# Four more attention pairs turned on VectorE instead of TensorE, in a kernel of attention and two feed-forward blocks

## The chip, the cores and the metric

The kernel runs on one core of a Trainium2 chip. The metric is the device time of one execution in microseconds, here the median of a few runs. The core has a matrix engine (TensorE, PE in the profile), three engines for elementwise work (VectorE is DVE, ScalarE is ACT, GpSimd is POOL) and DMA queues, which this kernel drives from SyncE (SP). Each engine works through its own instructions in a fixed order and waits on semaphores for what the others make.

## What is computed

```python
# attention: B, H, S, D = 4, 12, 448, 64, causal
scores = scale * np.matmul(q, k.transpose(0, 1, 3, 2))
scores = np.where(mask, -1000000000.0, scores)
scores = scores - np.max(scores, axis=-1, keepdims=True)
attn = np.exp(scores)
attn = attn / (np.sum(attn, axis=-1, keepdims=True) + 1e-09)
out = np.matmul(attn, v)
# x: 1792 tokens x 768
h = (x @ w1) * (x @ w2) @ w3          # 768 -> 1024 -> 1024
x = h @ w_out                         # 1024 -> 768
h = x @ w_in                          # 768 -> 2048
g = h - np.tanh(h)
out = g @ moe2_w_out                  # 2048 -> 768
```

All of it is in float32. The kernel forms w3 @ w_out once ("the product") and uses that for the second step.

## The kernel before

Large products keep each operand as two rounded parts, hi and lo, and take three matmuls for each step of the contraction (L411 to L413). `split` (L272) makes the parts: a cast gives hi on ScalarE or VectorE, and a subtraction gives lo on GpSimd or VectorE.

The work of attention goes by pairs of heads: a pair (b, p) is heads 2p and 2p + 1 of batch b, and there are six pairs in a batch. Two forms are in use. In the **first form** (`attention`, L432) TensorE makes the scores (L488) in chunks of 112 queries, VectorE adds the mask and finds the maximum (L459), ScalarE takes the exponential (L501), TensorE turns the probabilities by 20 matmuls with the identity (L513), they are copied out of PSUM to the tiles `pt`, TensorE multiplies with v (L541) and spreads the reciprocal sums (L548). The result goes through `xp` (L552, L554) and `split` (L557) into `x`, the input of the bilinear product. In the **turned form** (`turned`, L569) the scores (L657) come in two groups with rows of 64 to 448 columns, VectorE reduces (L603), ScalarE takes the exponential (L620), ScalarE or VectorE scales with the reciprocal (L629, L631), VectorE turns blocks of 32 x 32 (L633), and TensorE multiplies with v by 100 small matmuls in row groups of 32 (L683), which stand in two halves in the order. v is kept four times, once for each row group.

Before the change, the 12 pairs of batches 0 and 1 are in the first form and the 12 of batches 2 and 3 in the turned one; the outputs of batches 2 and 3 are stored to DRAM (`scx`, L700) and fetched in the second half of the kernel. The tiles of the turned form take the place of those of the first (the pools `at` and `bt`), so the first of them waits for the end of all first-form pairs.

Beside attention, TensorE works on one long sequence of other matmuls: the product (`product`, tiles mm<-g,hl), then, for the tokens of batches 0 and 1, the bilinear product with w1 and w2 (`bilinear`, L780, tiles mm<-x,hl) in blocks of 384 and 512 tokens (`BLOCKS`), then `project` (L816). The block of 384 needs x of batch 0 alone, the block of 512 x of both batches. Each step k of the contraction needs the x of pair k of the batch. The weights for these come raw from DRAM and are converted by `convert` (L288) on ScalarE, VectorE and GpSimd; `jobs_12` are w1 and w2, and the first `EARLY` = 4 tiles of w_in are converted in this first stage too.

The order of all this is made by a planner when the kernel is built (`Plan`, L89): each step has a rank and an estimated cost, and the step that can start first is taken. Pairs have ranks by their number, the long sequence has the last rank and fills what is left. On the chip only the order remains, with semaphores.

After this first half, the second half of the tokens and the two steps with w_in and w_out follow, in the same manner.

Of the kernel before, what the change touches and what calls it, by code (L numbers as in the profile page):

```python
# [25 lines left out]
B, H, S, D = 4, 12, 448, 64  # L26
NT, DM, FF, FF2 = 1792, 768, 1024, 2048
P = 128
CH = 112
NCH = S // CH  # L30
NKB = S // 32
NP = H // 2

EARLY = 4
W = 2 * S

# [17 lines left out]
def block(a, c):  # L54

    return (a if a < 2 else None) if c == 0 else 4 * c - 2 + a


def tokens():

    return [32 * block(a, c) + i for a in range(4) for c in range(4) if block(a, c) is not None for i in range(32)]

# [133 lines left out]
def act(n, psum=False):  # L198
    return "ACT", (0.104 if psum else 0.147) + n / 1400
# [31 lines left out]
def dma(size):  # L231
    return "DMA", max(0.5, size / 330e3)
# [3 lines left out]
def body(ctx: ExitStack, tc: tile.TileContext, qkd, vd, vd4, w12, w3t, wo, w_in, wo2, out):  # L236
    nc = tc.nc
    V, A, G, SP, PE = nc.vector, nc.scalar, nc.gpsimd, nc.sync, nc.tensor
    PSUM = bass.MemoryType.PSUM
    plan = Plan()  # L240
# [31 lines left out]
    def split(n, hi, lo, x):  # L272

        copy((yield [act(n), dve2(n)]), hi, x)
        sub((yield [pool(n), dves(n)]), lo, x, hi.bitcast(F32))
# [109 lines left out]
    scx = [dram.tile([P, W], F32, name=f"scx_{p}") for p in range(NP)]  # L385
# [43 lines left out]
    x_ready = grid(4, NP)  # L429
    spilled = grid(2, NP)  # L430

    def attention(at, aps, x_a):  # L432
        pairs = [(b, p) for b in range(2) for p in range(NP)]
        r_qk = Ring(at, [P, 2, S], F32, "qk", 2)
        r_v = Ring(at, [CH, NCH, 2, D], F32, "v", 2)
        r_p = Ring(at, [CH, 2, 1120], F32, "p", 2)
# [5 lines left out]
        qks, qk_at = {}, [Event() for _ in pairs]  # L442
        vs, v_at = {}, [Event() for _ in pairs]
        over = [Event() for _ in pairs]

        def load(ring, tiles, events, src):
            for n, (b, p) in enumerate(pairs):
                tiles[n] = yield ring
                yield dma(4 * P * 8 * D if tiles is vs else 4 * P * W)
                SP.dma_start(out=tiles[n].t, in_=src[b, p])  # L450
                plan.set(events[n])

        def scaled(p, st, chunks, ps, event):
# [112 lines left out]
        return over  # L566


    def turned(at, aps, pps):  # L569
        pairs = [(b, p) for b in range(2, B) for p in range(NP)]  # L570
        r_qk = Ring(at, [P, 2, S], F32, "qk", 3)
        r_v = Ring(at, [P, NKB, 2, D], F32, "v", 2)
        r_p = Ring(at, [P, 2, PLACE[-1]], F32, "p", 2)
# [2 lines left out]
        r_xb = Ring(at, [P, S], F32, "xb", 2)  # L576
        r_sc = Ring(aps, [P, 2, 512], F32, "sc", 1)
        r_pv = Ring(pps, [P, 4, 512], F32, "pv", 1)
        qks, qk_at = {}, [Event() for _ in pairs]
        vs, v_at = {}, [Event() for _ in pairs]  # L580
        over = [Event() for _ in pairs]

        def load(ring, tiles, events, src, first):
            for n, (b, p) in enumerate(pairs):
                tiles[n] = yield ring
                yield dma(4 * P * NKB * 2 * D if tiles is vs else 4 * P * W)
                SP.dma_start(out=tiles[n].t, in_=src[b - first, p])
                plan.set(events[n])

        def soft(p, pt, st, chunks, ps, rank, left, event):  # L590
# [46 lines left out]

        def pair(n):
            b, hp = pairs[n]
            rank = 24 + 2 * n  # L640

            yield qk_at[n]
            qk = qks.pop(n)
            p = yield r_p
            sb = yield r_st
            pt = yield r_pt
            left, event = [2 * 4], Event()
            for group in ((3, 0), (2, 1)):
                ps = yield r_sc
                yield wide(sum(WIDE[c] for c in group), 2)  # L650
                chunks, o = [], 0
                for c in group:
                    w = WIDE[c]
                    q0 = max(0, P * c - D)
                    for e in range(2):
                        d = slice(e * D, (e + 1) * D)
                        PE.matmul(ps.t[:, e, o:o + w], qk.t[d, 0, q0:q0 + P], qk.t[d, 1, :w], start=True, stop=True)  # L657
                    chunks.append((c, o))
                    o += w
                plan.spawn(soft(p, pt, sb.t, chunks, ps, rank, left, event), rank)  # L660
            plan.done(qk)

            yield event
            plan.done(p)
            plan.done(sb)
            yield v_at[n]
            v = vs.pop(n)
            ps = yield r_pv
            for kb in range(NKB):
                if kb in (0, 6):  # L670

                    if kb:
                        plan.pause(4.0)
                    yield "PE", 1.4
                for a in range(4):
                    have = [c for c in range(4) if block(a, c) is not None and block(a, c) >= kb]
                    if not have:
                        continue
                    r = slice(32 * a, 32 * a + 32)
                    for e in range(2):  # L680
                        src = pt.t[r, e, have[0] * STEP + kb * 32:]
                        x = bass.AP(tensor=src.tensor, offset=src.offset, ap=[src.ap[0], [STEP, len(have)], [1, 32]])
                        PE.matmul(ps.t[e * D:(e + 1) * D, a, have[0] * 32:P], v.t[r, kb, e], x,  # L683
                                  start=kb == 0, stop=kb == block(a, 4 - 1))
            plan.done(pt)
            plan.done(v)
            tk = slice((b % 2) * S, (b % 2 + 1) * S)

            def parts(t):

                return (t[:, :256].rearrange("p (a n) -> p a n", a=2), t[:, 256:].rearrange("p (a n) -> p a n", a=2))
            out = ps.t[:, 0:2, :P], ps.t[:, 2:4, 32:P]
            xb = yield r_xb
            o = parts(xb.t)
            for i in range(2):
                yield act(S // 2, True)
                A.copy(out=o[i], in_=out[i])
            plan.done(ps)
            yield dma(P * S * 4)
            SP.dma_start(out=scx[hp][:, tk], in_=xb.t)  # L700
            plan.set(spilled[b - 2][hp])
            plan.done(xb)
            plan.set(over[n])

        plan.spawn(load(r_qk, qks, qk_at, qkd, 0), 24)
        plan.spawn(load(r_v, vs, v_at, vd4, 2), 25)
        for n in range(len(pairs)):
            plan.spawn(pair(n), 24 + 2 * n)
        return over


# [275 lines left out]

    def start(cv, r_raw, r_t, at, aps):
        x = yield r_x
        xa["over"] = attention(at, aps, x.t)  # L990
        plan.spawn(first_half(cv, r_raw, r_t, x), plan.FILLER)
        plan.set(spawned)
# [9 lines left out]
        plan.run(xa["over"])  # L1002
    with tc.tile_pool(name="bt", bufs=1) as bt, tc.tile_pool(name="bps", bufs=1, space=PSUM) as bps, \
            tc.tile_pool(name="bpp", bufs=1, space=PSUM) as bpp:
        over = turned(bt, bps, bpp)
        plan.run([l1_over])
        plan.run(over + [j.stored for j in jobs_12 + jobs_in[:EARLY]] + sum(ab_ready[0], []))
    cv.__exit__(None, None, None)
# [105 lines left out]
```

## Time and profile before

| | before |
|---|---|
| median of 3 runs | 1066.53 us (1063.65 to 1068.56) |
| the profiled execution | 1062.6 us |
| its span | 1060.8 us |
| TensorE (PE) busy | 1036.4 us, 98% |
| VectorE (DVE) busy | 643.3 us, 61% |
| ScalarE (ACT) busy | 619.4 us, 58% |
| GpSimd (POOL) busy | 242.5 us, 23% |

The profile is of one execution, and its span is the time from the first to the last instruction; the execution's own time has 1.8 us more around it. The share of an engine is its busy time over the whole span. The chain that ended last is followed back from the last instruction, at each step to what released it; its pieces follow one another and add up to the span. Matmuls are pipelined, so the duration of one in a list is longer than the distance to the next.

### The profile page before, as it was taken

To read this page: it belongs to the slowest core of one execution; us is meant where nothing else is said; L and a number is where in the kernel's file an instruction comes from. 1 tells how busy PE (TensorE), PEld (TensorE's weight loads), DVE (VectorE), ACT (ScalarE), POOL (GpSimd) and SP (SyncE) were. 2 spreads that over 40 slices of the span, in tenths; PEclk is the share of its full clock that TensorE was granted. 3 is DMA by queue.
4 is the path that set the end of the run, shared out by engine and by line. 5 is a ranking of instruction groups with operands and counts; after the bars stand their busy time and mean duration, and the time that the engine had idled before them with its cause. 6 is when DMAs were issued, how large, how long until landed. Compare 5 with 4: busy or idle time off the path is not lost.

```text
span 1060.8 us, 19813 instructions
## 1 busy us (share of the span) xinstructions
PE 1036.4 (98%) x7680; PEld 899.3 (85%) x7680; DVE 643.3 (61%) x1316; ACT 619.4 (58%) x1353; POOL 242.5 (23%) x188
## 2 busy tenths in 40 slices
PE   5799999999999999999999999999999999999998
PEld 3577788778888989888998989899888988988987
DVE  7886556667665466656565377384756655474742
ACT  6997868788776243433432488573736556553620
POOL 3542131222223400124532022121111111121210
PEclk8999999999999999999999999999999999999999
DMA  7674449877764798999998333233333543233124
GB/s 265 205 215 161 121 149 315 298 255 253 251 223 159 295 366 301 347 323 319 354 326 300 142 118 119 90 129 109 109 110 117 167 140 115 92 120 117 44 87 155
DMA packets 72318, 209.03 MB, mean 197 GB/s; under 512 B 6113, under 2 KB 21473, under 8 KB 70689
## 3 DMA queue, kind: packets, MB, share of 16 engines
q1 hardware_dynamic: 72224, 207.77, 57.0%
q8 instruction: 60, 0.98, 0.4%
q14 instruction: 34, 0.27, 0.1%
HBM read 155.45 MB, written 52.30 MB: 196 GB/s over the span
## 4 chain that ended last, share of the span: by engine, by line
PE 91%; ACT 3%; DMA 2%; DVE 2%; issue 1%; POOL 0%; SPq 0%; ACTq 0%; DVEq 0%
PE mm L411 28%; PE mm L413 27%; PE mm L412 27%; PE pv L683 3%; PE sc L657 2%; PE att L541 1%; DMA raw<-w3t 1%; ACT p L501 1%; PE att L488 1%; PE att L513 1%; ACT pt L267 1%; ACT raw L304 1%; DVE p L459 1%; DMA qk<-qkd 1%; DVE t L321 0%
## 5 line engine op out<-in xcount | busy, mean ns | idle before, releaser
L411 PE MATMUL mm<-x,hl 128*128 128x384 f32 (+1 forms) x768 | 282.1, 367 | 0.0
L413 PE MATMUL mm<-x,hl 128*128 128x384 f32 (+1 forms) x768 | 278.8, 363 | 0.0
L412 PE MATMUL mm<-x,hl 128*128 128x384 f32 (+1 forms) x768 | 278.6, 363 | 0.0
L270 POOL TENSOR_TENSOR g<-g 128x384 fp32r<-128x384 f32 (+1 forms) x64 | 76.7, 1199 | 371.1 <-ACT g L267 371.1
L411 PEld LDWEIGHTS mm<-x,hl 128*128 128x128 f32 x768 | 144.1, 188 | 18.7 <-issue 2.0
L413 PEld LDWEIGHTS mm<-x,hl 128*128 128x128 f32 x768 | 144.1, 188 | 15.3
L412 PEld LDWEIGHTS mm<-x,hl 128*128 128x128 f32 x768 | 144.2, 188 | 14.7
L413 PE MATMUL mm<-g,w 128*128 128x384 f32 (+1 forms) x384 | 139.6, 364 | 0.0
L412 PE MATMUL mm<-g,w 128*128 128x384 f32 (+1 forms) x384 | 139.4, 363 | 0.0
L411 PE MATMUL mm<-g,w 128*128 128x384 f32 (+1 forms) x384 | 139.1, 362 | 0.0
L897 DVE SCALAR_TENSOR_TENSOR g<-r,g 128x512 f32<-128x512 f32 (+1 forms) x192 | 124.7, 659 | 20.4 <-ACT r L888 17.6
L888 ACT ACTIVATE r<-sq,cst 128x384 f32<-128x384 f32 (+1 forms) x192 | 123.6, 666 | 8.0 <-DVE g L897 8.0
L411 PE MATMUL mm<-g,hl 128*128 128x384 f32 (+1 forms) x320 | 116.3, 363 | 2.1 <-POOL g L270 2.1
L413 PE MATMUL mm<-g,hl 128*128 128x384 f32 (+1 forms) x320 | 113.0, 353 | 0.0
L412 PE MATMUL mm<-g,hl 128*128 128x384 f32 (+1 forms) x320 | 112.9, 353 | 0.0
L881 DVE SCALAR_TENSOR_TENSOR g<-sq,mm 128x384 f32<-128x384 f32 (+1 forms) x64 | 39.6, 619 | 109.2 <-ACT th L879 108.6
L314 DVE TENSOR_SCALAR t<-raw 128x512 uint32<-128x512 uint32 (+1 forms) x80 | 52.3, 654 | 69.6 <-DMA raw<-wo 39.1
L875 ACT ACTIVATE sq<-mm 128x384 f32<-128x384 f32 (+1 forms) x64 | 34.7, 543 | 92.5 <-PE mm L413 92.4
L304 ACT ACTIVATE raw<-raw 128x512 uint32<-128x512 uint32 (+1 forms) x80 | 63.9, 799 | 33.7 <-DMA raw<-wo 16.3
L270 POOL TENSOR_TENSOR hl<-t,hl 128x512 fp32r<-128x512 f32 (+1 forms) x32 | 52.1, 1635 | 134.0 <-ACT hl L267 99.1
L321 DVE CUSTOM_DVE_ANT_0 t<-raw,t 128x1024 uint16<-128x1024 uint16 (+1 forms) x80 | 75.1, 938 | 6.7 <-ACT raw L304 0.2
L412 PEld LDWEIGHTS mm<-g,w 128*128 128x128 f32 x384 | 72.1, 188 | 8.0
(81 smaller groups left out, 1599.0 us busy)
## 6 DMA issues: line engine op xcount, KB each, us to landing
hl<-sci SPq DMA_DIRECT2D x32, 768.0 KB, 4.6
w<-sco SPq DMA_DIRECT2D x48, 512.0 KB, 3.5
raw<-w SPq DMA_DIRECT2D x16, 768.0 KB, 5.7
sc<-hl SPq DMA_DIRECT2D x16, 768.0 KB, 4.4
raw<-w_in SPq DMA_DIRECT2D x16, 768.0 KB, 6.7
hl<-scp SPq DMA_DIRECT2D x12, 1024.0 KB, 6.5
hl<-sc SPq DMA_DIRECT2D x16, 768.0 KB, 7.0
raw<-wo SPq DMA_DIRECT2D x24, 512.0 KB, 6.7
```

Of the source, the lines that this page charges most:

```text
L270: (V if eng == "DVE" else G).tensor_tensor(out=out, in0=in0, in1=in1, op=ALU.subtract)
L304: A.activation(out=u, in_=u, func=AF.Copy, scale=2.0 ** -29)
L314: V.tensor_scalar(out=t, in0=raw[:, :n, 1], scalar1=3, scalar2=0x3FFFFFF8, op0=ALU.logical_shift_left, op1=ALU.bitwise_and)
L321: V.tensor_tensor(out=t, in0=t, in1=raw[:, :n, 0], op=ALU.add)
L411: PE.matmul(ps, wh, xl, start=k == 0, stop=False)
L412: PE.matmul(ps, wl, xh, start=False, stop=False)
L413: PE.matmul(ps, wh, xh, start=False, stop=k == last)
L683: PE.matmul(ps.t[e * D:(e + 1) * D, a, have[0] * 32:P], v.t[r, kb, e], x, start=kb == 0, stop=kb == block(a, 4 - 1))
L875: A.activation(out=sq, in_=h, func=AF.Square)
L881: V.scalar_tensor_tensor(out=g, in0=sq, scalar=LEAD, in1=h, op0=ALU.mult, op1=ALU.mult)
L888: A.activation(out=rk.t[:, :n], in_=sq, func=AF.Square, bias=cst[:, k:k + 1])
L897: V.scalar_tensor_tensor(out=g, in0=rk.t[:, :n], scalar=QUAD[k][1], in1=g, op0=ALU.add, op1=ALU.mult)
```

## The change

The first form now takes the first eight pairs only (`FIRST = 8`: batch 0 and pairs 0 and 1 of batch 1), and the turned form takes the other sixteen. The four turned pairs of batch 1 write their output through `split` into `x`, as the first form does, and the others are stored as before. The copy of a turned output from PSUM now puts the tokens in their natural order (64 and 384 elements in place of 256 and 192), so that the host need not reorder its result. The input arrays `vd` and `vd4` are cut at pair 8 in place of batch 2.

```diff
+FIRST = 8
...
     def attention(at, aps, x_a):
-        pairs = [(b, p) for b in range(2) for p in range(NP)]
+        pairs = [(b, p) for b in range(B) for p in range(NP)][:FIRST]
...
-                SP.dma_start(out=tiles[n].t, in_=src[b, p])
+                SP.dma_start(out=tiles[n].t, in_=src[n] if tiles is vs else src[b, p])
...
-    def turned(at, aps, pps):
-        pairs = [(b, p) for b in range(2, B) for p in range(NP)]
+    def turned(at, aps, pps, x_a):
+        pairs = [(b, p) for b in range(B) for p in range(NP)][FIRST:]
...
-            rank = 24 + 2 * n
+            rank = 2 * (FIRST + n)
...
-            out = ps.t[:, 0:2, :P], ps.t[:, 2:4, 32:P]
-            xb = yield r_xb
-            o = parts(xb.t)
-            for i in range(2):
-                yield act(S // 2, True)
-                A.copy(out=o[i], in_=out[i])
-            plan.done(ps)
-            yield dma(P * S * 4)
-            SP.dma_start(out=scx[hp][:, tk], in_=xb.t)
-            plan.set(spilled[b - 2][hp])
+            xb = yield r_xb
+            yield act(D, True)
+            A.copy(out=xb.t[:, :D].rearrange("p (a n) -> p a n", a=2), in_=ps.t[:, :2, :32])
+            yield act(S - D, True)
+            A.copy(out=xb.t[:, D:].rearrange("p (c a n) -> p a c n", a=4, n=32),
+                   in_=ps.t[:, :, 32:P].rearrange("p a (c n) -> p a c n", n=32))
+            plan.done(ps)
+            tk = slice((b % 2) * S, (b % 2 + 1) * S)
+            if b < 2:
+                yield from split(S, x_a[:, 0, hp, tk], x_a[:, 1, hp, tk], xb.t)
+                plan.set(x_ready[b][hp])
+            else:
+                yield dma(P * S * 4)
+                SP.dma_start(out=scx[hp][:, tk], in_=xb.t)
+                plan.set(spilled[b - 2][hp])
...
-        "vd": v[:2].reshape(2, NP, 2, NCH, CH, D).transpose(0, 1, 4, 3, 2, 5),
-        "vd4": np.tile(v[2:].reshape(2, NP, 2, NKB, 32, D).transpose(0, 1, 4, 3, 2, 5), (1, 1, 4, 1, 1, 1)),
+        "vd": v.reshape(B * NP, 2, NCH, CH, D)[:FIRST].transpose(0, 3, 2, 1, 4),
+        "vd4": np.tile(v.reshape(B * NP, 2, NKB, 32, D)[FIRST:].transpose(0, 3, 2, 1, 4), (1, 4, 1, 1, 1)),
```

Line numbers in the changed kernel are lower by 3 in the functions concerned (L411 is L408, L657 is L654, L683 is L680, L267 is L264, L620 is L617). Two places of the order matter below. The first is TensorE, where the first block of 512 tokens of the bilinear product begins (mm_2188 before). Before the change it stands between the first and the second turned pair of batch 2:

```order
L683 MATMUL pv_2009<-pt_1761,v_1745 64x32 x20
L411 MATMUL mm_2093<-x_163,hl_1809 128x384
L412 MATMUL mm_2093<-x_163,hl_1809 128x384
L413 MATMUL mm_2093<-x_163,hl_1809 128x384
L411 MATMUL mm_2188<-x_163,hl_1809 128x512
L412 MATMUL mm_2188<-x_163,hl_1809 128x512
L413 MATMUL mm_2188<-x_163,hl_1809 128x512
L683 MATMUL pv_2191<-pt_1778,v_1813 64x128 x4
```

In the changed order the block is mm_2106; its steps k = 0 to 4 stand between the output groups of the moved pairs, and this is its last step, k = 5, behind the last output of the fourth moved pair (pv_2187, which is pair 5 of batch 1) and one group of scores of a later pair:

```order
L680 MATMUL pv_2187<-pt_1892,v_1893 64x32 x20
L654 MATMUL sc_2344<-qk_1829 128x448 x2
L654 MATMUL sc_2344<-qk_1829 128x64 x2
L408 MATMUL mm_2106<-x_163,hl_1618 128x512
L409 MATMUL mm_2106<-x_163,hl_1618 128x512
L410 MATMUL mm_2106<-x_163,hl_1618 128x512
L408 MATMUL mm_2367<-x_163,hl_1812 128x512
```

What moved: the last step of the block reads x of a pair whose output is made directly ahead of it. The second place is ScalarE, where the x of pair 5 of batch 1 is cast to its hi part. Before, that is the first form (xp_1710), ahead of all turned pairs:

```order
L304 ACTIVATE raw_1619<-raw_1619 128x768
L552 COPY xp_1710<-att_1678 128x448
L267 CAST x_163<-xp_1710 128x448
L750 CAST res_1756<-mm_1686 128x384
L750 CAST res_1811<-mm_1755 128x384
L620 ACTIVATE p_1759,st_1760<-p_1759,st_1760 128x448 x2
```

In the changed order it is the turned form (xb_2335), among the exponentials (L617) and scalings (L626) of the next pair:

```order
L617 ACTIVATE p_1986,st_1988<-p_1986,st_1988 128x320 x2
L617 ACTIVATE p_1986,st_1988<-p_1986,st_1988 128x192
L687 COPY xb_2335<-pv_2187 128x64
L617 ACTIVATE p_1986,st_1988<-p_1986,st_1988 128x192
L689 COPY xb_2335<-pv_2187 128x4x3x32
L607 ACTIVATE st_1988<-st_1988 128x4
L264 CAST x_163<-xb_2335 128x448
```

What moved: the copies and the cast of this x are interleaved with the softmax of the next pair, and the subtraction for lo stays on GpSimd.

## Rows read from the trace of the kernel before

**Rows 1.** The page: its span, busy time by engine, and the chain by engine.
```profile
span 1060.8 us, 19813 instructions
...
PE 1036.4 (98%) x7680; PEld 899.3 (85%) x7680; DVE 643.3 (61%) x1316; ACT 619.4 (58%) x1353; POOL 242.5 (23%) x188
...
PE 91%; ACT 3%; DMA 2%; DVE 2%; issue 1%; POOL 0%; SPq 0%; ACTq 0%; DVEq 0%
```

**Rows 2.** What TensorE waited for, 95 to 345 us: total us, times, longest.
```profile
PE pv L683 <- issue: 1.0, 2, 0.7
```

**Rows 3.** The chain, 113 to 133 us, first form: start us, us, what.
```profile
116.58 1.92 PE att L513 x20
118.49 0.20 PE mm L411
...
119.56 2.08 PE att L488 x16
121.64 0.37 PE mm L411
122.01 0.17 PE mm L412
...
122.36 2.04 PE att L541 x16
124.40 0.53 PE att L548 x4
```

**Rows 4.** The chain, 206 to 236 us, turned form.
```profile
209.00 1.45 PE pv L683 x60
210.46 0.37 PE mm L411
...
216.56 0.43 PE mm L411
216.99 0.23 PE mm L412
...
217.46 1.12 PE sc L657 x8
...
223.19 1.06 PE sc L657 x8
```

**Rows 5.** Groups by line and form: busy us, mean ns, then idle before.
```profile
L620 ACT ACTIVATE p<-p,st 128x192 f32<-128x192 f32 x24 | 10.8, 449 | 2.3 <-DVE st L603 2.3
...
L270 POOL TENSOR_TENSOR x<-xp,x 128x448 fp32r<-128x448 f32 x12 | 15.7, 1311 | 51.5 <-ACT x L267 51.5
...
L267 ACT CAST x<-xp 128x448 fp32r<-128x448 f32 x12 | 6.9, 571 | 2.8 <-DVE xp L554 2.8
...
L697 ACT COPY xb<-pv 128x256 f32<-128x256 f32 x12 | 4.4, 370 | 3.9 <-PE pv L683 3.8
...
L697 ACT COPY xb<-pv 128x192 f32<-128x192 f32 x12 | 3.8, 317 | 0.0
```

**Rows 6.** The timeline of ScalarE and of GpSimd: start us, us, instruction, idle before.
```profile
152.76 0.57 ACT L267 CAST x<-xp 128x448 fp32r<-128x448 f32 x1 [0.69 <-DVE xp L554]
153.41 1.79 POOL L270 TENSOR_TENSOR x<-xp,x 128x448 fp32r<-128x448 f32 x1 [0.83 <-ACT x L267]
```

**Rows 7.** What ScalarE waited for, 95 to 360 us.
```profile
ACT raw L304 <- DMA raw<-w: 3.7, 3, 3.1
```

**Rows 8.** Windows of 1 us: length, PE busy, granted clock, DMA share, GB/s.
```profile
18.00:19.00 1.00, 0.04 (x2) 0.58 0.32 129
...
24.00:25.00 1.00, 1.00 (x5) 0.51 0.29 49
...
39.00:40.00 1.00, 0.00 (x0) 1.00 0.90 362
```

**Rows 9.** The chain: first output of the first turned pair, last of the fourth.
```profile
180.11 1.45 PE pv L683 x60
...
227.24 1.37 PE pv L683 x81
```

More of the change, by code (lines that the diff above doesn't have):

```diff
@@ L56, in block @@
     return (a if a < 2 else None) if c == 0 else 4 * c - 2 + a
-def tokens():
-    return [32 * block(a, c) + i for a in range(4) for c in range(4) if block(a, c) is not None for i in range(32)]
 class Event:
@@ L581, in turned, with load @@
         over = [Event() for _ in pairs]
-        def load(ring, tiles, events, src, first):
+        def load(ring, tiles, events, src):
             for n, (b, p) in enumerate(pairs):
@@ L586, in load @@
                 yield dma(4 * P * NKB * 2 * D if tiles is vs else 4 * P * W)
-                SP.dma_start(out=tiles[n].t, in_=src[b - first, p])
+                SP.dma_start(out=tiles[n].t, in_=src[n] if tiles is vs else src[b, p])
                 plan.set(events[n])
@@ L686, in pair @@
             plan.done(v)
-            tk = slice((b % 2) * S, (b % 2 + 1) * S)
-            def parts(t):
-                return (t[:, :256].rearrange("p (a n) -> p a n", a=2), t[:, 256:].rearrange("p (a n) -> p a n", a=2))
-            out = ps.t[:, 0:2, :P], ps.t[:, 2:4, 32:P]
-            xb = yield r_xb
-            o = parts(xb.t)
-            for i in range(2):
-                yield act(S // 2, True)
-                A.copy(out=o[i], in_=out[i])
-            plan.done(ps)
-            yield dma(P * S * 4)
-            SP.dma_start(out=scx[hp][:, tk], in_=xb.t)
-            plan.set(spilled[b - 2][hp])
+            xb = yield r_xb
[5 more added lines that the diff above has]
+            plan.done(ps)
+            tk = slice((b % 2) * S, (b % 2 + 1) * S)
+            if b < 2:
[5 more added lines that the diff above has]
+                plan.set(spilled[b - 2][hp])
             plan.done(xb)
             plan.set(over[n])
-        plan.spawn(load(r_qk, qks, qk_at, qkd, 0), 24)
-        plan.spawn(load(r_v, vs, v_at, vd4, 2), 25)
+        plan.spawn(load(r_qk, qks, qk_at, qkd), 2 * FIRST)
+        plan.spawn(load(r_v, vs, v_at, vd4), 2 * FIRST + 1)
         for n in range(len(pairs)):
-            plan.spawn(pair(n), 24 + 2 * n)
+            plan.spawn(pair(n), 2 * (FIRST + n))
         return over
@@ L989, in start @@
         x = yield r_x
+        xa["x"] = x.t
         xa["over"] = attention(at, aps, x.t)
@@ L1004, in body @@
             tc.tile_pool(name="bpp", bufs=1, space=PSUM) as bpp:
-        over = turned(bt, bps, bpp)
+        over = turned(bt, bps, bpp, xa["x"])
         plan.run([l1_over])
@@ L1111 @@
     o = r.results[0]["out"]
-    o = o.transpose(2, 0, 1).reshape(B, S, DM)
-    return np.concatenate([o[:2], o[2:, np.argsort(tokens())]]).reshape(NT, DM)
+    return np.ascontiguousarray(o.transpose(2, 0, 1).reshape(NT, DM))
```

## The prediction

> **What bounds the kernel now.** I read four things, in this order. The head of the page [rows 1] shows TensorE busy for 98% of the span and 91% of the chain that ended last; VectorE and ScalarE, by the same rows, work about six tenths of the time. A share over the whole span hides stages, so the second view is what TensorE waited for between 95 and 345 us, the stretch that holds the last attention pairs and all pairs that VectorE turns [rows 2]: 1.0 us of pauses in issue, ahead of two groups of pv matmuls, is the one entry that touches the turned pairs. In that stretch the span is the sum of what TensorE is given to do, and a microsecond of matmuls taken away is a microsecond of span as long as no wait appears. Third, the chain in that stretch gives the time that each kind of step takes of TensorE [rows 3, 4, 9]; its durations run from the start of one step to the start of the next, so they may be added, unlike the means of the page, which overlap. Fourth come the pieces off TensorE from which a new wait would be made [rows 5 to 7], and the granted clock after gaps [rows 8]. Before 95 us TensorE does wait, but the changed kernel issues the same matmuls in the same order until the output of pair 5 (counted from 0), so I carry that stretch over unchanged; and behind the last pv group the instructions of TensorE are again the same to the end.
>
> **The matmuls removed and added.** A pair in the first form costs TensorE 2.08 us of scores, 1.92 of transposes, 2.04 of output and 0.53 for the reciprocals [rows 3]: 6.57 us. A turned pair costs 1.12 + 1.06 of scores [rows 4] and 1.45 + 1.37 of output [rows 9]: 5.00 us. For four pairs the difference of 1.57 us is 6.3 us. But the steps around them are not free. The first matmul of a 128-row product behind scores or a turned output takes 0.37 us where the next of its kind takes 0.17, or 0.43 against 0.23 for 512 columns; behind the transposes it takes 0.20 [rows 3, 4]. So each return from a group with narrow tiles costs 0.20 us. A first-form pair has one such return (its scores; the output is followed by the full-row transposes of the reciprocals): 6.77 us. In the changed order I count 14 returns for the 16 groups of the four moved pairs, 2.8 us or 0.70 a pair: 5.70 us. The saving is 1.07 us a pair, 4.3 us for four. Its ends are 6.3 (returns free) and about 4.
>
> The Trainium skill has a rule that speaks against the change here: "TensorEngine Tiling (Array Packing)", Key Properties, says that a change of tiling mode drains TensorE. By that rule every added group is charged; the rows agree, with 0.20 us at each return; without it the saving would be put at 6.3 us.
>
> **The new wait.** The four moved pairs are pairs 2 to 5 of batch 1, and their x is no longer there early. In the changed order the product w_out by w3 is used up when pair 4 of batch 1 is at its output; the first 512-column block of the bilinear product needs the x of every pair of batch 1, k after k, and its last step, k = 5, stands behind the last pv group of pair 5 with one group of scores (1.12 us) between. Before, the last subtraction that makes this x began at 153.41 us [rows 6], long before the first turned output at 180.11 [rows 9]. What must happen between is: two copies out of PSUM, 0.37 + 0.32 us (the new copies have other shapes, 64 and 384 elements, but the same 448 in all); one exponential of the next pair that stands between them on ScalarE, 0.45; one small correction of the sums, which I estimate at 0.1; the cast to hi, 0.57; and GpSimd's subtraction, 1.31 in the mean [rows 5]. That is 3.1 us; a hand-over took 0.08 (a cast that ended at 153.33, a subtraction that began at 153.41 [rows 6]), and with four of them it is 3.4. ScalarE will also be some 0.6 us behind, because the last exponentials of the next pair stand ahead of the first copy. Less the 1.1 us of scores, TensorE stands for 2.9 us. The lower end is 0 (the scores are held up so that copies are done when they end); the upper end adds ScalarE's wait for a raw weight, of which the stretch had three, 3.1 us the longest [rows 7]: one such load's pass stands in ScalarE's queue ahead of these copies. So 0 to 6 us. The steps k = 0 to 4 need pairs that are done at least 5 us of TensorE's work earlier; no charge. Behind the waiting matmul only TensorE's own queue is held: the output of the first pair of batch 2, which is then not ready much sooner.
>
> GpSimd's subtraction is bounded by rows too: 1.31 us in the mean, but 1.79 for the one at 153.41 us, when VectorE worked on a raw weight [rows 5, 6]; VectorE has the same kind of work queued near the new subtraction, so 0.5 us more is within the bounds above.
>
> The Trainium skill's "SBUF — State Buffer", Who interferes with whom, has VectorE and GpSimd share one port pair that the loser waits for. The 1.79 us agrees with it; by that rule the wait would be 3.4 us instead of 2.9.
>
> **What I cost at nothing.** ScalarE's and VectorE's extra work for the moved pairs (transposes on VectorE, scaling on ScalarE) lies beside product matmuls, of which the changed order has 108 of 384 columns between the first and the last output group of the four; when these run out the cover is gone, which is the wait above. The four-fold v is 896 KB a pair in place of 224, by the shapes; it is asked for behind the first qk, over 15 us of TensorE's work before its use. The start of the turned phase, where the queue of loads waits for GpSimd's last x of the first form, has 42 product matmuls as cover where it had 45: up to 0.5 us, taken as 0. The pauses in issue [rows 2] came where output groups lay close; the moved pairs lie as close, and I add 0.3 us (0 to 1).
>
> **The sum.** -4.3 + 2.9 + 0.3 = -1.1 us. The profiled execution took 1062.6 us (span 1060.8 and 1.8 around it): 1061.5. The median of the three runs is 1066.5, 3.9 above it, so the forecast for a median is 1065.4 us. A measurement of this kernel can tell about 0.5%, 5.3 us, from no change; the three runs alone spread over 4.9 us.
>
> **Rivals.**
>
> *No wait.* The x of pair 5 comes in time, and the saving of 4.3 us stays, or up to 6.3 if the returns overlap better: a median of 1060.2 to 1062.2. For it: in this stretch TensorE waited for no result of a turned pair. Against: the order leaves 1.1 us for a chain of 3.4. Chance 0.16.
>
> *The clock falls in the gap.* In the microsecond from 18 us TensorE was busy for 0.04 us and the granted clock fell, to a mean of 0.58; it stood at half, 1.2 GHz, until 25 us [rows 8], which takes 3.4 us of work from a full TensorE (0.42 + five times 0.5 + 0.49). From 39 to 40 us TensorE was not busy at all and the clock stayed whole [rows 8]. The new gap, some 0.8 us ahead of the scores and 2 behind them, may be of either kind. Then -1.1 + 3.4 = +2.3, a median of 1068.8. Chance 0.2.
>
> *The softmax engines can't keep the pace, and the kernel is slower.* From the first output group of the first turned pair to the end of the fourth's last, the old trace takes from 180.11 to 227.24 + 1.37, 48.5 us [rows 9]. The changed order gives the four moved pairs less: 108 matmuls of 384 columns at 0.17 us and 15 of 512 at 0.23 make 21.8, six score groups 6.5, eight output groups 11.3, thirteen returns 2.6: 42.2 us. If ScalarE and VectorE need 48.5, the wait at k = 5 grows by 6.3: +5.2, and with the clock's 3.4 +8.6: medians of 1071.7 to 1075.1. For it: the distance shrinks by an eighth. Against: in the old 48.5 us TensorE was never late, so the engines may have had time left. It makes the kernel slower from 1.1 us of added lateness of the fourth moved pair on, and measurably so from 6.4, or from 3.0 where the clock falls too. Chance 0.14.
>
> That the change does not move the work is excluded: the instructions hold 16 turned pairs and 8 of the first form.
>
> **Chances and range.** The forecast has 0.5. Faster by over 0.5% (below 1061.2) is the better part of the first rival and a little scatter: 0.16. Slower by over 0.5% (above 1071.9) is most of the last rival and scatter on the second: 0.13. Within: 0.71. The range goes from 1060, the foot of the first rival, to 1071.5, the head of the clock's case with a scatter of some 2.5 us; it leaves out most of the last rival.
>
> **What would show it.** Right: scores, transposes and pv at the durations of [rows 3, 4]; TensorE idle for 2 to 4 us ahead of the last k-step of the first 512-column product, released by GpSimd's x; and all that stands behind the last turned output about 1 us earlier. Wrong: no such wait and a span 4 us shorter; a granted clock of half in the microseconds behind the wait; pv groups of the moved pairs waiting for VectorE's transposes; or a wait at the start of the turned phase for qk.

## The result and the profile after

The changed kernel is slower: a median of 1073.36 us in 11 runs (1067.67 to 1076.77) against 1066.53 us in 11 runs of the kernel before (1062.95 to 1070.05), a ratio of 1.006 with a 95% interval of 1.0042 to 1.0078. The forecast was 1065.4 us, its range ended at 1071.5, and "slower by over 0.5%" had a chance of 0.13. The profiled execution took 1074.12 us.

The head of its page, with the granted clock by slices and the chain:

```profile
span 1072.3 us, 21159 instructions
...
PE 1038.4 (97%) x8320; PEld 900.5 (84%) x8320; DVE 651.2 (61%) x1349; ACT 622.5 (58%) x1376; POOL 239.2 (22%) x188
...
PEclk9999999899999999999999999999999999999999
...
PE 78%; DMA 2%; DVE 1%; POOL 0%; ACT 0%; issue 0%; SPq 0%; DVEq 0%; ACTq 0%
```

Beside [rows 1] the shares look alike: TensorE fell from 98% to 97%. The chain's 78% for TensorE, where it was 91%, can't be set beside the old share: this chain is followed back only to 192 us, and its shares add up to 81%. What TensorE waited for between 95 and 360 us (total us, times, longest) shows where time was lost; "issue" is time in which TensorE stood and waited for nothing that the profile shows:

```profile
PE pv L680 <- issue: 2.1, 2, 1.1
PE mm L408 <- POOL x L267: 1.8, 1, 1.8
PE sc L654 <- DMA qk<-qkd: 1.0, 1, 1.0
PE sc L654 <- DVE st L600: 0.6, 1, 0.6
```

In [rows 2] the first of these was the only entry that touched a turned pair. Between 360 and 620 us, where before TensorE waited for no engine, there is now:

```profile
PE mm L408 <- POOL g L267: 2.7, 1, 2.7
```

**The step k = 5.** The timeline of ScalarE, GpSimd and TensorE around the predicted wait (start, us, instruction, idle before):

```profile
189.07 0.46 ACT L617 ACTIVATE p<-p,st 128x192 f32<-128x192 f32 x1 [0.41 <-DVE st L600]
189.53 0.19 ACT L687 COPY xb<-pv 128x64 f32<-128x64 f32 x1
189.62 0.46 ACT L617 ACTIVATE p<-p,st 128x192 f32<-128x192 f32 x1
190.07 0.46 ACT L689 COPY xb<-pv 128x384 f32<-128x384 f32 x1
190.43 0.21 ACT L607 ACTIVATE st<-st 128x4 f32<-128x4 f32 x1
190.56 0.56 ACT L264 CAST x<-xb 128x448 fp32r<-128x448 f32 x1
...
191.21 1.13 POOL L267 TENSOR_TENSOR x<-xb,x 128x448 fp32r<-128x448 f32 x1 [10.08 <-ACT x L264]
...
189.37 1.19 PE L654 MATMUL sc<-qk 64*128 64x448 f32 x8 [0.62 <-DVE st L600]
192.39 0.79 PE L408 MATMUL mm<-x,hl 128*128 128x512 f32 x1 [1.83 <-POOL x L267]
```

This is the predicted chain, instruction by instruction. TensorE had 0.62 us of idling ahead of the scores and 1.83 behind them. What followed is in windows of 1 us (length, busy time of PE, PEld, DVE, ACT and POOL, granted clock, DMA share, GB/s):

```profile
190.00:191.00 1.00, 0.56 (x8) 0.24 (x4) 0.33 (x2) 1.00 (x5) 0.00 (x0) 1.00 0.67 244
191.00:192.00 1.00, 0.00 (x0) 0.00 (x0) 1.00 (x5) 1.00 (x4) 0.80 (x1) 0.59 0.90 373
192.00:193.00 1.00, 0.61 (x2) 0.51 (x3) 1.00 (x4) 1.00 (x4) 0.34 (x1) 0.50 0.59 222
...
197.00:198.00 1.00, 1.00 (x62) 1.00 (x52) 0.54 (x2) 0.89 (x2) 0.00 (x0) 0.50 0.20 77
198.00:199.00 1.00, 1.00 (x50) 0.81 (x39) 0.00 (x0) 0.81 (x3) 0.00 (x0) 0.99 1.02 399
```

The clock fell in the gap and stood at half, 1.2 GHz, for 6.8 us: from a full TensorE that takes 3.4 us of work. Some 1.2 us of it lay in the gap itself, where there was nothing to slow down, so it is nearer to 2.8 here. The rival that had a chance of 0.2 is what happened.

**The turned pairs.** The chain behind it (start, us, what) shows the steps at the durations of [rows 3, 4, 9]:

```profile
203.23 1.37 PE pv L680 x82
204.60 0.38 PE mm L408
205.85 1.12 PE sc L654 x8
206.97 0.37 PE mm L408
...
211.33 1.45 PE pv L680 x60
212.79 1.06 PE sc L654 x8
```

**The second half.** The wait for g at the end of the second bilinear product, again by timelines:

```profile
546.17 0.62 ACT L264 CAST cvo<-t 128x512 fp32r<-128x512 f32 x1 [3.39 <-DMA sco<-cvo]
546.70 0.51 ACT L264 CAST g<-asb 128x384 fp32r<-128x384 f32 x1
...
548.10 1.18 POOL L267 TENSOR_TENSOR g<-asb,g 128x384 fp32r<-128x384 f32 x1
...
549.33 0.49 PE L408 MATMUL mm<-g,hl 128*128 128x384 f32 x1 [2.69 <-POOL g L267]
```

ScalarE stood 3.39 us for a store of a converted weight (`cvo`), and the cast of the last g was queued behind that. In the kernel before, ScalarE has the two casts of g first and the weight's cast behind them; its timeline there:

```profile
537.37 0.51 ACT L267 CAST g<-asb 128x384 fp32r<-128x384 f32 x1 [2.65 <-DVE asb L801]
538.36 0.62 ACT L267 CAST cvo<-t 128x512 fp32r<-128x512 f32 x1 [0.47 <-DMA sco<-cvo]
```

TensorE's order is the same in both; ScalarE's isn't. Behind this wait, too, the changed kernel has half clock, here in a window of 1 us (columns as above):

```profile
551.00:552.00 1.00, 1.00 (x4) 0.71 (x4) 0.56 (x1) 0.50 (x1) 0.42 (x1) 0.50 0.34 88
```

The first matmul of the first projection starts at 368.72 us, where it was 362.31; from there to the end of the span it is 703.5 us, where it was 698.5.

### The profile page after: what moved, and what is told of

The parts are those of the page before. It is cut to its first block, busy times and chain, and to the rows that moved or that the text cites. A ratio compares the mean times of both kernels' runs of the same rounds, so it can differ in the third digit from the quotient of the medians.

```text
span 1072.3 us, 21159 instructions
## 1 busy us (share of the span) xinstructions
PE 1038.4 (97%) x8320; PEld 900.5 (84%) x8320; DVE 651.2 (61%) x1349; ACT 622.5 (58%) x1376; POOL 239.2 (22%) x188
## 4 chain that ended last, share of the span: by engine, by line
PE 78%; DMA 2%; DVE 1%; POOL 0%; ACT 0%; issue 0%; SPq 0%; DVEq 0%; ACTq 0%
PE mm L408 25%; PE mm L410 24%; PE mm L409 24%; PE pv L680 3%; PE sc L654 2%; DMA raw<-wo 1%; DMA sco<-cvo 1%; POOL cvo L267 0%; DVE t L318 0%; DVE t L311 0%; DVE t L314 0%; ACT cvo L264 0%; POOL g L267 0%; SPq L372 0%; DVE acc L929 0%
## 5 line engine op out<-in xcount | busy, mean ns | idle before, releaser
L408 PE MATMUL mm<-x,hl 128*128 128x384 f32 (+1 forms) x768 | 283.5, 369 | 1.9 <-POOL x L267 1.8
L408 PEld LDWEIGHTS mm<-x,hl 128*128 128x128 f32 x768 | 144.5, 188 | 21.6 <-issue 2.7
L267 POOL TENSOR_TENSOR g<-g 128x384 fp32r<-128x384 f32 (+1 forms) x64 | 76.8, 1199 | 371.5 <-ACT g L264 371.5
L408 PE MATMUL mm<-g,w 128*128 128x384 f32 (+1 forms) x384 | 139.1, 362 | 0.0
L408 PE MATMUL mm<-g,hl 128*128 128x384 f32 (+1 forms) x320 | 117.3, 367 | 4.5 <-POOL g L267 4.5
L311 DVE TENSOR_SCALAR t<-raw 128x512 uint32<-128x512 uint32 (+1 forms) x80 | 54.5, 682 | 65.8 <-DMA raw<-wo 33.3
L267 POOL TENSOR_TENSOR hl<-t,hl 128x512 fp32r<-128x512 f32 (+1 forms) x32 | 51.9, 1628 | 144.8 <-ACT hl L264 97.5
L409 PEld LDWEIGHTS mm<-g,w 128*128 128x128 f32 x384 | 72.1, 188 | 8.0
L408 PEld LDWEIGHTS mm<-g,w 128*128 128x128 f32 x384 | 72.1, 188 | 7.9
```

The costliest lines, as they stand in the source:

```text
L267: (V if eng == "DVE" else G).tensor_tensor(out=out, in0=in0, in1=in1, op=ALU.subtract)
L311: V.tensor_scalar(out=t, in0=raw[:, :n, 1], scalar1=3, scalar2=0x3FFFFFF8, op0=ALU.logical_shift_left, op1=ALU.bitwise_and)
L408: PE.matmul(ps, wh, xl, start=k == 0, stop=False)
L409: PE.matmul(ps, wl, xh, start=False, stop=False)
```

## The experiments

Two stretches are kept apart in what follows: the first half, up to the first matmul of the projection, and the rest of the span behind it, the second half. The clock's loss is the span times (1 - mean granted clock), meaned over the runs of a kernel: 9.8 us in the changed kernel, 6.5 to 7.3 in the kernel before in the four sessions of the experiments. The profile that the prediction was made from, with a mean clock of 0.997, had lost only 3.

The theories at the start: **1**, two separate losses, the gap with its clock (5.2 us) and the late wait for g (4.6 us with its clock); **2**, the first half alone; **3**, the moved pairs themselves.

### First four

e1_late puts a weight's buffer 2 us later in the planner; TensorE's order stays.

```diff
+SLOW = 2.0
...
             SP.dma_start(out=j.scratch, in_=j.buf.t[:, :, :j.n].bitcast(F32))
+            plan.now += SLOW if j.n == 512 else 0.0
             plan.done(j.buf)
```

> One part of the first half is left as in the changed kernel; only the planner's idea of when a buffer of a converted w_out tile of the second feed-forward block is free again is put 2 us later, so that ScalarE's queue at the end of the second bilinear product has the cast of the last g ahead of the cast of a weight, as before the change, and not behind it. Theory 1 (two losses: a gap of 1.9 us and then 6.8 us at half clock, 3.4 us of work, behind the fourth moved pair, 5.2 us together; and 2.7 us of waiting with some 2 us of clock at 549 us, 4.6 us together): the second loss goes, 1073.4 - 4.6 = 1068.8 us, no wait of TensorE for g between 520 and 560 us, the gap at the first 512-column block stays. Theory 2 (all of the loss is in the first half; the wait at 549 us was an accident of one run): 1073.4 us, and the wait may be absent in any run. Theory 3 (the moved pairs themselves cost more: pauses in issue and returns from narrow tiles): 1073.4 us.

Measured: 1071.15 us (ratio to before 1.0034, 1.0016 to 1.0053). The wait for g at 549 us is gone, as theory 1 had it, but not its price. Between 360 and 660 us there now stood, in its profile:

```profile
PE mm L410 <- DVE asb L801: 1.5, 3, 0.8
PE mm L410 <- DVE x L268: 1.2, 1, 1.2
```

e2_fill reorders the first blocks (j, w1 or w2, block); e3_fill_late adds the edit of e1; e4_none_moved is the changed kernel with one number changed.

```diff
+AHEAD = [(0, 0, 0), (0, 1, 0), (1, 0, 0), (0, 0, 1), (0, 1, 1), (1, 1, 0), (1, 0, 1), (1, 1, 1)]
...
-        for j in range(8):
-            for s in range(2):
-                for t in there_and_back():
+        todo = [(j, s, t) for j in range(8) for s in range(2) for t in there_and_back()]
+        if xr is x_ready_first:
+            todo[:8] = AHEAD
+        for i, (j, s, t) in enumerate(todo):
```

> The changed kernel with the first eight blocks of the bilinear product in another order: three blocks of 384 columns, which need batch 0 alone, come ahead of the first block of 512. Some 7.7 us of matmuls and scores now stand between the last output of the fourth moved pair and the step that needs its x, where 1.1 us stood. The planner's order at the end of the second bilinear product also falls back to the old one (the cast of g ahead of the weight's). Theory 1 (both losses): both go, 1073.4 - 5.2 - 4.6 = 1063.6 us, no wait for x at the first 512-column block, clock whole there. Theory 2 (first half only): 1073.4 - 5.2 = 1068.2 if the gap is all of it. Theory 3 (the moved pairs themselves, or VectorE and ScalarE too late with them): 1073 us, or a wait for x that is as long although 6.6 us more lie ahead of it.

> As the run before, and the planner's idea of a free buffer put 2 us later as well, which here has the opposite effect on ScalarE's order: the cast of the last g stands behind the cast of a weight again. Theory 1: the first loss is gone, the second is there: 1063.6 + 4.6 = 1068.2 us, with a wait for g of 2 to 3 us ahead of the second half's projection. Theory 2 and theory 3: the same time as the run before.

> FIRST = 12: no pair is moved, only the copies of the turned outputs to their natural order (64 and 384 elements) and the new cut of the arrays are left of the change. All theories above: 1066.5 us within 1.5 us, since the order of all engines is that of before. A fourth theory, that the new copies (three dimensions, short runs of 32) hold up ScalarE: above 1068 us, with copies longer than 0.37 and 0.32 us.

Measured: e2 1070.24 us (1.0028, 1.001 to 1.0045), e3 1071.31 (1.0042, 1.0024 to 1.0059), e4 1067.32 (1.0001, 0.9985 to 1.0017). The new copies cost nothing, to within the 1.7 us of e4's interval. In e2 the gap is gone and the clock's loss is back at 7.5 us, yet 6.6 us of the forecast gain are missing. Again waits stood in the second half where the kernel before has none and e4 has 0.2 us:

```profile
PE mm L409 <- DVE x L268: 1.5, 2, 0.8
PE mm L409 <- POOL g L268: 1.1, 1, 1.1
```

So the loss in the second half isn't one wait: take one away and others come.

### Second four

e5_fill_slow and e6_after_slow apply `SLOW = 1.5` to every stored weight, with and without the reordered blocks; e7_two_moved has `FIRST = 10`; e8_pause8 is e5 with `plan.pause(8.0)` in place of 4.0 between the halves of an output.

> As e2_fill, and the planner takes a buffer of any converted weight that is stored to be free 1.5 us later, so that at the end of both bilinear products ScalarE's queue has the casts of the last two g ahead of a weight's cast (in e2_fill the first product's end had a w_in cast, late for its buffer, ahead of the last g, and TensorE waited 1.1 us for g and 1.5 for x in the projection behind it). If the time that e2_fill still loses against before is such waits behind late weight casts: 2.4 us under e2_fill, about 1068 us, no waits of TensorE between 360 and 560 us. If it is the moved pairs' own cost: as e2_fill, 1070 to 1071 us.

> The changed kernel with its own order of blocks (the gap of 1.8 us and the clock behind it stay) and only the buffers' time moved by 1.5 us as in e5: both ends of the bilinear products have the g casts first. If gap and clock (5.2 us) stand by themselves beside the late casts: 5.2 us over e5_fill_slow, about 1073 us if the pauses are alike, and the half clock for 3.4 to 6.8 us behind the gap. If the order of blocks in e2 and e5 worked by something else: no difference between e5 and e6.

> FIRST = 10: only pairs 4 and 5 of batch 1 move. Behind the last output of the second moved pair stand 9 matmuls of 512 columns and a group of scores (3.2 us) ahead of the step that needs its x, against a chain of 3.7 us. Theory 1 (work saved, minus gap and clock, minus late casts): work -2.1 us, gap 0.5 us, no clock lost, casts in the old order, pauses in issue up by 0.5 to 1: 1066.5 us. If every moved pair costs more than it saves, whatever stands behind it: above 1069 us.

> As e5_fill_slow, with the two halves of a turned output kept 8 us apart by the planner in place of 4: the second half of one pair and the first of the next now stand closer together (52 and 48 small matmuls with 6 matmuls of 384 columns and one group of scores between), and the halves of one pair farther apart. If TensorE's pauses in issue come of small matmuls that use up instructions faster than they are loaded, they sit behind such clusters and grow to over 5 us in all, each ending 1 to 1.5 us behind a load of 16 KB in the queue of instruction loads; time 2 us or more over e5. If the pauses are by chance and independent of the spacing: the same time as e5 within 1 us.

Measured: e5 1067.58 us (1.000, 0.9981 to 1.002), as forecast. e6 1067.54 (1.0007, 0.9991 to 1.0023), 5.5 under its forecast: with the same order of TensorE as the changed kernel, the same gap of 1.8 us in its profile and 3.4 us at half clock behind it, it is 5.8 us faster than that. Only the order on the other engines differs, and that only from 355 us on: up to there ScalarE, VectorE and GpSimd have the order of the changed kernel. That moved the question from the gap to the second half. Part of the 5.8 us is the clock, whose loss in e6 is 7.8 us where the changed kernel has 9.8. What stays odd is that e5, whose gap is filled, isn't faster than e6: its projection began 2.6 us earlier in the profiles (362.1 and 364.7), but the medians are equal.

e7 1066.17 us (0.9992, 0.9972 to 1.0012), within 0.4 us of the forecast: two moved pairs cost nothing that these runs can tell (the interval goes from 3.0 us faster to 1.3 slower). e8 1065.09 (0.998, 0.9965 to 0.9995), 2.5 us under e5 where 2 or more above was expected. Its pauses in issue came to 0.2 us, with the clusters of small matmuls closer together; in their place output groups waited 2.2 us for ScalarE's copies out of PSUM. The theory that such clusters make the pauses fell with it. In 16 profiles they vary from none to 6.7 us, in kernels of the same order of TensorE from 1.3 to 3.7 (the changed one, e1, e6, e9, e13), and what sets their number and length stays open (where they end is told in the last section).

### Third four

e9_again is the changed kernel unaltered. e10_none_moved_late has `FIRST = 12` with `SLOW = 4.0` for 512-column weights, which gives ScalarE the swap of casts seen at 546 us. e11_none_moved_slow and e12_none_moved_slow_pause8 are e6 and e8 without moved pairs (and without reordered blocks).

> The changed kernel once more, unaltered, in the session of the three runs below. If the late wait belongs to the order of ScalarE (a weight's cast, late for its buffer, ahead of the last g), TensorE waits for g again for 2 to 3 us near 549 us, and the gap for x of 1.8 us near 190 us is there again; time 1072 to 1073.5 us. If either was an accident of one run, it is not there.

> No pair is moved (as e4_none_moved, 1067.3 us), TensorE's order is that of e4, and only the planner's idea of the buffers of w_out of the second block is put 4 us later, which here puts a weight's cast ahead of the cast of the last g at the end of the second bilinear product, the order that the changed kernel has. If that order is what costs the changed kernel its second loss: a wait for g near 545 us, 2.5 to 4.5 us over e4, 1070 to 1072 us. If the second loss needs the moved pairs: 1067.3 us.

> No pair is moved, and the buffers' time of e5 and e6 (1.5 us later for every stored weight). The control of e6: if the later buffers only take away what the change had brought (late casts), the kernel with no pair moved doesn't gain: 1067 us, and the moved pairs are worth nothing beside it. If the later buffers help any order: 1064 to 1065 us, and the moved pairs still cost some 3 us.

> As e11, with the halves of a turned output 8 us apart. The control of e8_pause8 (1065.1 us): if the distance of the halves is what made e8 faster, 2 us under e11, about 1065 us or less; if e8 was faster by the moved pairs, with their gap filled and their casts in order: as e11, 1067 us.

Measured: e9 1071.74 us (1.0038, 1.0012 to 1.0065). The gap of 1.8 us is there again. The waits of the second half are there too, but spread out, though no instruction differs:

```profile
PE mm L409 <- DVE asb L800: 0.9, 2, 0.7
PE mm L409 <- DVE x L268: 0.9, 1, 0.9
PE mm L409 <- POOL g L268: 0.7, 1, 0.7
```

e10 1067.36 us (0.9999, 0.9984 to 1.0013) with no wait of TensorE at all between 360 and 660 us. In ScalarE's order the weight's cast does stand ahead of the last g:

```profile
537.11 0.62 ACT L265 CAST cvo<-t 128x512 fp32r<-128x512 f32 x1
539.53 0.51 ACT L265 CAST g<-asb 128x384 fp32r<-128x384 f32 x1 [1.80 <-DVE asb L801]
```

But here that cast waited for no store, and with the swap many other instructions moved, from 482 us on. So the swap costs nothing where the buffer is free; a cast that has to wait for its store, ahead of the last g, wasn't tested without the moved pairs. The theory of the single cast is weakened rather by e9, which has the very order of the changed kernel: there the same cast stood 0.87 us for its store, where it was 3.39, and TensorE waited 0.7 us for g, where it was 2.7, while the median is only 1.6 us lower. e11 1069.45 (1.0019, 1.0006 to 1.0031): the later buffers don't help every order, they cost the kernel without moved pairs 2.0 us; under that setting the moved pairs (e6) are the faster ones by 1.9 us in the medians, and by 1.3, give or take 2.1, in the ratios to the kernel before. e12 1068.60 (1.0013, 0.9995 to 1.0031): the distance of the halves isn't what made e8 fast. The same change, then, is worth -1.9 us in one setting of the planner, which is not clear of nothing, and +4.3 to +6.8 in the other.

### The last two

The planner's state where the first half ends showed why. The second half is planned from there. In the kernel before, that point falls at step k = 2 of the projection's second product; in the changed one it falls one step earlier, with a subtraction still pending, and from such a start all later choices come out otherwise. e13_after_old_second and e14_fill_old_second hold the second half fixed:

```diff
-        plan.run(over + [j.stored for j in jobs_12 + jobs_in[:EARLY]] + sum(ab_ready[0], []))
+        plan.run(over + [j.stored for j in jobs_12 + jobs_in[:EARLY]] + sum(ab_ready[0], []) + [gate])
+        plan.free = {e: plan.free["PE"] + d for e, d in {'PE': 0.0, 'ACT': -1.0, 'DVE': -0.42, 'POOL': -0.47, 'DMA': 1.91}.items()}
+        plan.port = plan.free["POOL"]
```

`gate` is set when the projection reaches that step. Behind it all five engines have the order of the kernel before, to the last instruction.

> The changed kernel, unaltered up to the projection of the first half (gap and clock at the first 512-column block included); there the planner's clocks of the five engines are set to the offsets that they have in the kernel before, one step of the contraction later, so that from there on every engine has the very order of the kernel before. If the re-planned second half is what costs 3 to 4.5 us of the measured 4.3 to 5.3: the changed kernel's 1071.7 to 1073 less some 3.7 us, 1068.5 us, and no waits of TensorE between 385 and 560 us. If the later waits come of the moved pairs themselves (their outputs 8 us later, more transfers), not of the order: 1071.7 us, with waits in those places again.

e14 also has, for j = 0, the blocks in the order 384 of w1, 384 of w2, 512 of w1, 512 of w2.

> As e13, and the bilinear product's second block of 384 columns (w2) ahead of its first two of 512: 9 matmuls of 512 columns and a group of scores, 3.2 us, stand between the last output of the fourth moved pair and the step that needs its x, against a chain of 3.7 us. If the gap costs what the profile of the changed kernel shows (1.9 us and 1.7 to 3.4 us of clock) and the second half now has its old order: 3 to 4.5 us under e13, about 1064.5 us, clearly under the 1067.5 us of the kernel before. If the gap is worth less (its work is lost again elsewhere in the first half): as e13 within 1.5 us.

Measured: e13 1069.09 us (1.0015, 0.9999 to 1.0031), e14 1064.85 us (0.9981, 0.9962 to 1.0001); forecast were 1068.5 and 1064.5. Between 95 and 360 us e13's first half waits as the changed kernel's does:

```profile
PE pv L680 <- issue: 3.0, 2, 1.6
PE mm L408 <- POOL x L267: 1.8, 1, 1.8
PE sc L654 <- DVE st L600: 0.6, 1, 0.6
PE sc L654 <- DMA qk<-qkd: 0.3, 1, 0.3
```

and between 360 and 660 us there is no wait left, in e13 none at all, in e14 only 0.4 us of issue. The table puts the kernels beside each other (first half and second half from one profiled execution each, clock's loss meaned over the runs):

| kernel | second half's order | first half, us | second half, us | clock's loss, us | median, us |
|---|---|---|---|---|---|
| before | old | 362.3 | 698.5 | 6.5 to 7.3 | 1066.53 to 1067.66 |
| e4, none moved | old | 369.7 | 699.5 | 7.5 | 1067.32 |
| changed | new | 368.7 | 703.5 | 9.8 | 1073.36 |
| e9, the same again | new | 368.3 | 702.2 | 9.5 | 1071.74 |
| e1 | its own | 369.6 | 702.3 | 9.4 | 1071.15 |
| e2, gap filled | its own | 364.1 | 702.2 | 7.5 | 1070.24 |
| e6 | its own | 364.7 | 700.3 | 7.8 | 1067.54 |
| e5, gap filled | its own | 362.1 | 700.7 | 6.8 | 1067.58 |
| e13 | old | 369.0 | 698.9 | 10.7 | 1069.09 |
| e14, gap filled | old | 368.2 | 699.2 | 7.7 | 1064.85 |

A single first half scatters by 7 us with the clock before 60 us and with the pauses (e4 and the kernel before have one order); the second half hardly scatters while nothing waits in it. With the old order it is 698.5 to 699.5, with the changed kernel's 702.2 and 703.5, with the orders of e1, e2, e5 and e6 700.3 to 702.3, and with e3's 705.4 (e8 can't be set beside them: two of its output groups fall behind the start of the projection). That the order costs this, and not the moved pairs, is shown by e13, and e6 agrees: both have the changed kernel's order on every engine up to 355 us or later. Their ratios lie 0.0045 and 0.0053 under the changed kernel's, give or take 0.0024, and 0.0023 and 0.0031 under e9's, give or take 0.0031, which alone would not be clear. Which of the order's many moves does it stays open. What the gap at k = 5 costs with its clock is less settled: filling it gave 4.2 us in e14 against e13, 0.9 in e2 against e1 and nothing in e5 against e6. e14 and e8 are the versions that come out under the kernel before, e8 with an interval that leaves out 1 (the only one of fourteen experiments on that side), e14 at the edge of what the runs tell.

## Why the prediction was wrong

**The matmuls: right.** Add the distances from the start of each matmul to the start of the next, without idling of over 0.15 us and with stretches at half clock counted half. The kernels with no pair moved (before, e4, e10) give 1033.1, 1034.7 and 1033.9 us; those with the order of the changed one or e14's (changed, e9, e13, e14) 1030.3, 1030.1, 1029.4 and 1029.1. The difference of the means is 4.2 us (4.1 to 4.4 with other limits for the idling, from 0.1 to 1 us), where 4.3 was predicted. The rule that I weighed there, "TensorEngine Tiling (Array Packing)", Key Properties, of the Trainium skill, has TensorE drain at a change of tiling mode; the 0.37 and 0.38 us of the returns to 128 rows above agree with it.

**The wait at k = 5: right in kind, 1.8 us with 0.6 ahead of it where 2.9 was put.** The subtraction took 1.13 us, not 1.31. The rule of "SBUF — State Buffer", Who interferes with whom, of the Trainium skill, by which VectorE could have held up GpSimd and made the wait 3.4 us, did not decide: VectorE was busy for all of the microsecond from 191, for the greater part with scores out of PSUM, and the subtraction was fast. The same section of the Trainium skill excepts a VectorE instruction with at most one SBUF input, outside the 2-port perf modes; the scores come from PSUM and only their mask from SBUF.

**The clock: the mechanism was named, but as a rival with 0.2.** It should have been in the sum. e13, where only this and small waits are left of the losses, came to 1069.09 us; the rival's time was 1068.8. Its price is 3.0 us by e13 against e14 (10.7 less 7.7), and 2.4 by the mean of the five kernels with the gap against the five with it filled (9.4 less 7.0), where 3.4 was written. It isn't a fixed price: with one order on every engine through the first 355 us, e6 lost 7.8 us to the clock and e13 10.7.

**The costs put at nothing.** The start of the turned phase was bounded by 0.5 us; in the changed kernel's profile it took 1.0, and 0.3 in e13. The way is the one described: the queue of loads issued qk only behind GpSimd's last x.

```profile
118.50 1.16 POOL L267 TENSOR_TENSOR x<-xp,x 128x448 fp32r<-128x448 f32 x1 [8.71 <-ACT x L264]
...
119.69 0.81 SPq L584 DMA_DIRECT2D qk<-qkd  x2
...
123.51 1.02 PE L654 MATMUL sc<-qk 64*128 64x448 f32 x4 [1.03 <-DMA qk<-qkd]
```

The pauses in issue, put at 0.3 with bounds of 0 and 1, were 1.7 us in the mean of the three profiles with no moved pair and the old order and 2.4 in the five with the order of the changed kernel: 0.7 more, within the bounds.

**The step that failed** is the sentence "behind the last pv group the instructions of TensorE are again the same to the end", from which the second half was carried over unchanged. The sentence is true and the conclusion wasn't. It looked at TensorE's order alone. On ScalarE, VectorE, GpSimd and in the queue of loads the second half was planned anew from a start one step earlier, and the new order has waits of TensorE where the old one has none: 2.7 us of waits in one profile, 2.5 in the next, and 2.7 to 4.3 us in the medians (1071.74 and 1073.36 against e13's 1069.09). Half clock stood behind such a wait in the changed kernel's profile alone, for 3.4 us from 549.6 on; e9, e1 and e2 have none in the second half. No rival had this. That the orders differ was to be seen before the run, on ScalarE from the first projection on, though not what the difference costs.

The rival of the softmax engines that can't keep the pace did not come: apart from 0.6 us for a maximum, no turned pair was waited for in the changed kernel. Measured against the sum: -4.3 + 2.4 (waits at k = 5) + 3.0 (clock) + 0.3 to 1.0 (start) + 0.7 (pauses) + 2.7 to 4.3 (second half) = 4.8 to 7.1 us, where the two sessions measured 4.3 and 6.8. The last term is taken from the same medians, so the agreement of the whole says little. Without it the sum is 2.1 to 2.8, beside 1.9 us for e13 (its interval goes from -0.1 to 3.3); that is what tests the other terms, and they fit within the scatter.

## What to carry to other kernels

Where a planner sets the order, compare the orders of all engines to the end of the program, not of the busiest one alone: a change in one stage re-plans all that follows, and a stage that had no waits can lose by it, as here, though it need not (e10). To learn what a change is worth in its own place, hold the rest of the order fixed, as e13 and e14 do; without that, the same change read as -1.9 us or as +6.8, and with it as +1.9 (e13), or -2.3 with the gap filled (e14). A wait of TensorE that may bring down the clock is to be priced with the clock behind it, as one term.

## What was not expected of the hardware

All five profiles with the gap at k = 5 (the changed kernel, e1, e6, e9, e13) have half clock behind its 1.8 us of idling, for 6.8 us in two and 3.4 us in three of them, with the same instructions on TensorE. e14, without that gap, has it behind a pause in issue, for which no engine is to blame. The first matmul behind that pause, and the windows around it:

```profile
185.31 0.40 PE L681 MATMUL pv<-pt,v 32*64 32x64 f32 x10 [1.88 <-issue]
```

```profile
184.00:185.00 1.00, 0.00 (x0) 0.00 (x0) 1.00 (x4) 0.00 (x0) 0.00 (x0) 1.00 0.92 355
185.00:190.00 5.00, 4.69 (x25) 4.39 (x25) 1.06 (x4) 2.86 (x8) 0.00 (x0) 0.66 0.87 331
```

Shorter pauses were followed by it or not: one of 1.1 us in e5 was, with half clock for 3.4 us, two of 1.1 us in the changed kernel were not. The fall also came late. In e13 the microsecond of full idling still had the whole clock, and the half clock stood when TensorE worked again:

```profile
192.00:193.00 1.00, 0.00 (x0) 0.00 (x0) 1.00 (x5) 1.00 (x3) 0.66 (x1) 1.00 0.97 409
...
194.00:195.00 1.00, 1.00 (x4) 0.77 (x3) 0.78 (x7) 0.66 (x3) 0.00 (x0) 0.50 0.02 7
...
197.00:198.00 1.00, 1.00 (x48) 0.68 (x52) 0.30 (x2) 0.76 (x3) 0.41 (x1) 0.82 0.00 0
```

Ahead of 60 us, where the kernel before and e4 have one order, the profile of the first shows no half clock between 30 and 60 us and that of the second two stretches of it. In 34 runs of the kernel before the clock's loss lay between 3.2 and 10.7 us: about half of the variance of those runs' times goes with it (a correlation of 0.69). The prediction was made from a profile at the low end of it.

The pauses in issue have a pattern that goes beyond this change. The page of the changed kernel lists a queue of instructions (packets, MB, share):

```profile
q8 instruction: 65, 1.06, 0.4%
```

Its packets are of 16 KB each, 60 to 65 in a span of 1060 to 1075 us. All 20 pauses in issue of 1 us and more behind 95 us, in thirteen of the profiles, end 1.2 to 1.6 us behind the end of such a packet; a shorter one, of 0.8 us in e11, doesn't. So it looks as if TensorE stood there for its own instructions. That is read from the traces and not tested: no run moved these packets, and why some come late stays open.
